# Retention and two feed-forward layers on one core: the order of the side work around the gated product's block products

## The chip, the cores and the metric

The kernel runs on one core of one Trainium2 chip. The metric is the device time of one execution in microseconds. Three runs of the kernel before took 1119.41 to 1124.32 us, with a median of 1120.45 us.

## The reference

A retention layer (linear attention whose state decays by a constant of each head) feeds two feed-forward layers, one with a leaky ReLU, one with a gate `h * sigmoid(1.702 h)`:

```python
for t in range(S):                       # S = 768, for 4 batches and 8 heads, head size 64
    state = gamma * state + einsum('bhd,bhe->bhde', k[:, :, t], v[:, :, t])
    y[:, :, t] = scale * einsum('bhd,bhde->bhe', q[:, :, t], state)
x = y.transpose(0, 2, 1, 3).reshape(3072, 512)
h = x @ moe_w_in;  x = maximum(0.01 * h, h) @ moe_w_out      # 512 -> 2048 -> 512
h = x @ moe2_w_in; x = (h * sigmoid(1.702 * h)) @ moe2_w_out
```

All is float32 in the result; the weights come in as float64 bit patterns and are made into float32 on the chip.

## The kernel before

Every value that TensorE multiplies stands as two parts, a rounded high part and a low part that is the rest, and each product is three matmuls (high by low, high by high, low by high). The order of the instructions on each engine is the order in which the program text issues them; no scheduler moves anything. Side work is put into a clock, `Later`: `at(ticks, step)` files a step, and each `tick()` at the end of a product runs the steps that are due.

The program has five stages, named here by the time at which the profiled execution is in them.

**Retention** (0 to 139 us) computes the first layer's input and the first of six token blocks of the first product.

**First product of the first layer** (139 to 356 us, `ffn_in`, L227): 5 blocks of 16 products, one tick each. Beside them 38 of 48 weight pieces are prepared. A `Prep` is one eighth-by-half of a weight matrix: it is loaded as 64-bit words; `words` makes float32 bits of them with two instructions on ScalarE (L167, L168) and four on VectorE (L169, L170, L172, L174); `sums` rounds (`round_up`, L178) and adds up three more block sums (L146); `store` writes seven blocks to DRAM. `Prep.start` files words, sums and store 3, 4 and 5 ticks behind the load. The raw words and the result take turns in three places.

**Second product of the first layer** (356 to 600 us, `Second`, L663): a Strassen-Winograd scheme with 7 block products instead of 8, in three token blocks of 56 items (7 products by 8 slices of the inner dimension). An item is 6 matmuls of 512 columns. Ahead of item n, `load` issues item n+13's data, `total` (L637) makes the operand sum of item n+5 on VectorE, `high` (L625, ScalarE) and `low` (L146, VectorE) split the operands of items n+4 and n+3. At the end of a product `evacuate` empties its PSUM banks: copies on ScalarE (L674, L684, L687, L704), sums on VectorE, and one sum on GpSimd (`other`, L671).

**Gated product, first of the second layer** (600 to 871 us, `First`, L497): the same scheme over 32 pairs (4 token blocks by 8 output slices); a pair is 7 block products of 6 matmuls with 384 columns, and a tick follows each product. For every pair ScalarE copies one accumulator to the other (L562), then a second one to SBUF (L568), and applies four sigmoids (L511); VectorE adds twice (L528) and multiplies four times (L515). The fourth product of a pair accumulates on the bank that L562 reads, and so waits for that copy. In the same stage stand `w_split` (L435, L146), which splits the weights of pairs 3 to 7, the remaining 10 `Prep`s (one at each even pair from 4 to 22), and for each new token block `early_sums` (L470, L471, on GpSimd) and seven `form`s (L483, L146).

**Second product of the second layer** (871 to 1121 us): `Second` again, with transposes of the results (L868).

What sets the order around the change is thus three tables: the ticks in `Prep.start`, the numbers in `LOADS, SUMS, HIGH, LOW`, and the pair and item numbers in `done1`, `step2`, `done2` and `done3`. The seven products of a pair that this document counts are those between two ticks of `First.run`.

## Time and profile before

| | |
|---|---|
| median of three runs | 1120.45 us |
| the profiled execution | 1122.98 us |
| its span, first to last instruction | 1121.3 us |
| mean granted TensorE clock | 0.987 |
| TensorE busy | 1070.3 us, 95% |
| VectorE busy | 835.0 us, 74% |
| ScalarE busy | 584.2 us, 52% |
| GpSimd busy | 74.3 us, 7% |

A row of the trace has the start of an instruction and its length in microseconds, its engine and line, and in square brackets the idle time of the engine before it and what ended that. In a table by stretches of time, the columns are the length of the stretch, the busy time of each engine with the count of its instructions, the granted TensorE clock as a share of full speed, the busy share of the DMA engines and what they moved. PEld is the load of weights into TensorE, which runs beside the matmuls.

### The profile page before, as it was taken

The numbers are of one execution on the slowest core, as the hardware profiler recorded it, in microseconds if no ns is written. First come the engines' busy times: TensorE is split into PE (matmuls) and PEld (weight loads), VectorE is DVE, ScalarE is ACT, GpSimd is POOL, SyncE is SP. The second block draws the span as 40 slices with busy tenths as digits, with TensorE's granted clock in tenths as the row PEclk, the third lists the DMA queues.
The fourth block names the chain that finished last, engine by engine and source line by source line (L and its number), as shares of the span: only waits on it lengthen the run. The fifth ranks groups of instructions, "written<-read, shape, count | busy, mean of one in ns | idle before, by whom it ended". The sixth has DMA issues, their size and how long they took to land.

```text
span 1121.3 us, 16864 instructions
## 1 busy us (share of the span) xinstructions
PE 1070.3 (95%) x6046; PEld 912.0 (81%) x6047; DVE 835.0 (74%) x1382; ACT 584.2 (52%) x1070; POOL 74.3 (7%) x45
## 2 busy tenths in 40 slices
PE   7999999999998999999988898988999999999997
PEld 5877788888887887878867897988899788888886
DVE  5988647977964887797887777585657897696784
ACT  5766444654556544545456553453556645545543
POOL 0211100000000000000023111011100000000000
PEclk9899999999999999999999999998999999999999
DMA  8899589998999328236255545454476725326322
GB/s 330 310 358 382 194 262 321 355 347 309 348 359 325 121 74 271 67 113 222 76 169 224 192 159 175 156 188 143 163 251 223 263 75 176 126 75 207 98 71 76
DMA packets 129636, 234.20 MB, mean 209 GB/s; under 512 B 11536, under 2 KB 69392, under 8 KB 126224
## 3 DMA queue, kind: packets, MB, share of 16 engines
q1 hardware_dynamic: 97152, 182.75, 48.3%
q10 hardware_dynamic: 32400, 50.38, 12.1%
q8 instruction: 47, 0.77, 0.3%
q14 instruction: 37, 0.30, 0.1%
HBM read 142.91 MB, written 90.18 MB: 208 GB/s over the span
## 4 chain that ended last, share of the span: by engine, by line
PE 74%; DVE 10%; DMA 7%; ACT 3%; issue 3%; POOL 1%; ACTq 1%; SPq 1%; DVEq 0%; POOLq 0%
PE psum L663 37%; PE psum L227 18%; PE psum L497 12%; PE psum L265 2%; DVE d L515 2%; DMA h<-qkv 2%; DMA h<-wd1o 2%; PE psum L295 1%; DMA h<-wd2o 1%; ACT h L435 1%; PE psum L868 1%; PE psum L288 1%; DVE c L146 1%; DVE e L146 1%; DMA gd<-d 1%
## 5 line engine op out<-in xcount | busy, mean ns | idle before, releaser
L663 PE MATMUL psum<-c,h 128*128 128x512 f32 x1008 | 232.5, 392 | 11.0 <-DVE c L146 11.0
L663 PEld LDWEIGHTS psum<-c,h 128*128 128x128 f32 x1008 | 189.7, 189 | 53.5 <-DVE c L146 14.2
L663 PE MATMUL psum<-e,h 128*128 128x512 f32 x810 | 192.5, 391 | 2.0 <-DVE e L146 2.0
L663 PEld LDWEIGHTS psum<-e,h 128*128 128x128 f32 x810 | 151.0, 188 | 34.7 <-DVE e L146 3.9
L497 PE MATMUL psum<-b,h 128*128 128x384 f32 x576 | 118.2, 351 | 19.0 <-ACT psum L562 18.6
L227 PE MATMUL psum<-d,h 128*128 128x512 f32 x576 | 135.9, 393 | 0.0
L227 PE MATMUL psum<-a,h 128*128 128x512 f32 x576 | 131.2, 389 | 0.0
L227 PEld LDWEIGHTS psum<-d,h 128*128 128x128 f32 x576 | 106.9, 188 | 24.8 <-issue 1.6
L227 PEld LDWEIGHTS psum<-a,h 128*128 128x128 f32 x576 | 108.0, 188 | 22.6 <-issue 0.2
L497 PEld LDWEIGHTS psum<-b,h 128*128 128x128 f32 x576 | 105.8, 198 | 23.5 <-ACT psum L562 23.5
L497 PE MATMUL psum<-c,h 128*128 128x384 f32 x576 | 112.1, 338 | 5.6 <-DVE psum L528 2.7
L497 PEld LDWEIGHTS psum<-c,h 128*128 128x128 f32 x576 | 102.0, 190 | 7.7 <-DVE psum L528 3.5
L511 ACT ACTIVATE d<-psum 128x384 f32<-128x384 f32 x96 | 47.2, 492 | 104.1 <-PE psum L497 58.2
L231 ACT ACTIVATE e<-psum 128x512 f32<-128x512 f32 x96 | 57.2, 595 | 80.3 <-PE psum L227 78.3
L625 ACT CAST c<-b 128x512 fp32r<-128x512 f32 x96 | 59.0, 622 | 67.7 <-DVE c L146 32.5
L146 DVE TENSOR_TENSOR h<-h 128x1024 fp32r<-128x1024 f32 (+3 forms) x51 | 52.5, 1037 | 48.5 <-ACT h L435 48.4
L146 DVE TENSOR_TENSOR c<-b,c 128x512 fp32r<-128x512 f32 x96 | 67.1, 702 | 14.8 <-ACT c L625 12.4
L625 ACT CAST e<-a 128x512 fp32r<-128x512 f32 x77 | 47.5, 622 | 51.5 <-DVE a L637 22.5
L146 DVE TENSOR_TENSOR e<-a,e 128x512 fp32r<-128x512 f32 x77 | 52.7, 688 | 14.5 <-ACT e L625 13.2
L435 ACT CAST h<-h 128x1024 fp32r<-128x1024 f32 (+3 forms) x51 | 45.2, 895 | 18.9 <-DMA h<-wd1o 4.2
L515 DVE TENSOR_TENSOR d<-psum,d 128x384 f32<-128x384 f32 x96 | 51.6, 551 | 4.5 <-ACT d L511 3.9
L663 PE MATMUL psum<-f,h 128*128 128x512 f32 x198 | 50.7, 391 | 0.0
(117 smaller groups left out, 1400.7 us busy)
## 6 DMA issues: line engine op xcount, KB each, us to landing
gd<-e ACTq DMA_DIRECT2D x96, 256.0 KB, 5.5
gd<-d ACTq DMA_DIRECT2D x128, 192.0 KB, 4.3
h<-qkv SPq DMA_DIRECT2D x21, 1024.0 KB, 7.6
b<-gd SPq DMA_DIRECT2D x72, 256.0 KB, 4.2
d<-gd SPq DMA_DIRECT2D x72, 256.0 KB, 4.5
a<-gd SPq DMA_DIRECT2D x48, 256.0 KB, 4.9
c<-w1i SPq DMA_DIRECT2D x16, 512.0 KB, 7.8
xd<-e SPq DMA_DIRECT2D x12, 512.0 KB, 3.1
```

The costliest lines, as they stand in the source:

```text
L146: e.tensor_tensor(out=o, in0=x, in1=y, op=ALU.subtract)
L227: nc.tensor.matmul(out=h, lhsT=w[:, a, k], rhs=xs[blk % 2][k][:, c], start=(i == 0), stop=(i == 3 * NP - 1), skip_group_check=True)
L231: nc.scalar.activation(out=t, in_=h, func=AF.Lrelu)
L265: nc.tensor.matmul(out=ps[:, e, n], lhsT=kT[r, n], rhs=qT[r, n], start=True, stop=True, skip_group_check=True)
L288: nc.tensor.matmul(out=kv[r, n], lhsT=ks[:, 2 * n + e], rhs=v[:, n, r], start=(c == 0 and n == 0), stop=True, skip_group_check=True)
L295: nc.tensor.matmul(out=out(n, e), lhsT=v[:, n, r], rhs=sm[:, e, n], start=(n < 2), stop=(c == 0), skip_group_check=True)
L435: nc.scalar.copy(out=hi.bitcast(F32R), in_=lo)
L497: nc.tensor.matmul(out=t, lhsT=w[:, k, a], rhs=x[:, b, k], start=(start and m == 0), stop=(m == 5), skip_group_check=True)
L511: nc.scalar.activation(out=s, in_=src, func=AF.Sigmoid, scale=1.702)
L515: nc.vector.tensor_tensor(out=dst, in0=src, in1=s, op=ALU.mult)
L625: nc.scalar.copy(out=t[:, 0], in_=self.block_of(*item))
L663: nc.tensor.matmul(out=t[:, j], lhsT=w[:, j, a], rhs=x[:, b], start=(new and q == 0 and m == 0), stop=(q == NQ - 1 and m == 2), skip_group ...
```

## The change

It touches five places.

1. In the gated product, weight splits and `Prep`s no longer run as whole steps of the clock. They are cut into pieces that stand in a queue, `behind`, and after each tick one piece is taken from it, except in a pair that forms operands of the next token block. A split is done by halves (`w_steps`), a `Prep` in six pieces (`steps`, `finish`), and its rounding and its three sums go from VectorE to GpSimd. Ten pairs are named for the ten `Prep`s.
2. In both second products the operand sums are issued from a table, `SUMS`, three in every four or five items, instead of eight in a row five items ahead. PSUM is emptied one to three items later than the end of its product, and the sum `other` moves from GpSimd to VectorE.
3. Six `Prep`s, those of the first three slices of the gated product's weights, are split when they are prepared, and both parts are stored (`wds`); their loads bring both parts, and they are not split again. All `Prep.start` ticks are one lower.
4. The operands of the gated product's first token block are formed a little earlier or later, with their sums on VectorE instead of GpSimd.
5. The last split of each second product stands at items 2 to 5 instead of 0 to 4, and by halves.

Where a `Prep` stands on VectorE in the gated product shows the first part. Here is VectorE before, from the `Prep` of pair 10 into pair 11 (pairs are counted from 0 to 31): L169 to L174 are `words`, L178 is `round_up`, the three L146 rows are the sums, and L528 and L515 are the pair's own adds and multiplies.

```order
L169 TENSOR_SCALAR e<-e 128x512
L170 TENSOR_SCALAR e<-e 128x512
L172 TENSOR_SCALAR e<-e 128x512
L174 SCALAR_TENSOR_TENSOR e<-e 128x512
L528 TENSOR_TENSOR psum<-psum,g 128x384
L178 ISA e<-e 128x1024
L146 TENSOR_TENSOR e<-e 128x256
L146 TENSOR_TENSOR e<-e 128x128 x2
L515 TENSOR_TENSOR d<-psum,d 128x384
L515 TENSOR_TENSOR d<-d 128x384
L515 TENSOR_TENSOR d<-psum,d 128x384 x2
```

And VectorE after, over pair 9, which has a `Prep` (L175 to L181 are the four `words`, L599 the adds, L586 the multiplies):

```order
L599 TENSOR_TENSOR d<-psum,g 128x384
L175 TENSOR_SCALAR e<-e 128x512
L177 TENSOR_SCALAR e<-e 128x512
L599 TENSOR_TENSOR psum<-psum,g 128x384
L586 TENSOR_TENSOR d<-psum,d 128x384
L586 TENSOR_TENSOR d<-d 128x384
L179 TENSOR_SCALAR e<-e 128x512
L181 SCALAR_TENSOR_TENSOR e<-e 128x512
L586 TENSOR_TENSOR d<-psum,d 128x384 x2
```

The pair's own instructions now stand between the words, one word to a tick, and the rounding and the sums are gone from VectorE.

They are on GpSimd, where before only the sums of the token blocks stood. GpSimd before, from the start of the gated product (L146 `form`'s sum, L470 and L471 `early_sums`):

```order
L146 TENSOR_TENSOR a<-a 128x768 x2
L470 TENSOR_TENSOR a<-a 128x768
L471 TENSOR_TENSOR a<-a 128x2x384
L146 TENSOR_TENSOR a<-a 128x768 x2
L470 TENSOR_TENSOR a<-a 128x768
L471 TENSOR_TENSOR a<-a 128x2x384
```

And after, from the third `Prep` before the second token block's sums (L190 is the rounding, L150 the sums of a `Prep` in tile e, L535 and L536 `early_sums`):

```order
L190 TENSOR_TENSOR e<-e 128x512
L150 TENSOR_TENSOR e<-e 128x256
L150 TENSOR_TENSOR e<-e 128x128 x2
L535 TENSOR_TENSOR a<-a 128x768
L536 TENSOR_TENSOR a<-a 128x2x384
L190 TENSOR_TENSOR e<-e 128x512
L150 TENSOR_TENSOR e<-e 128x256
L150 TENSOR_TENSOR e<-e 128x128 x2
L150 TENSOR_TENSOR a<-a 128x768 x2
```

A block's sums now queue behind the four GpSimd instructions of a `Prep` and before those of the next.

The third place is VectorE in the second product of the first layer, where the sixth product ends. Before (L637 an operand sum, L671 the emptying of PSUM, L146 `low`):

```order
L637 TENSOR_TENSOR b<-d,b 128x512
L671 TENSOR_TENSOR e<-psum,e 128x1024
L146 TENSOR_TENSOR c_3231<-b,c_3231 128x512
L637 TENSOR_TENSOR b<-d,b 128x512
L146 TENSOR_TENSOR c_3231<-b,c_3231 128x512
```

And after (L714 an operand sum, L748 the emptying, L150 `low`):

```order
L714 TENSOR_TENSOR b<-d,b 128x512
L748 TENSOR_TENSOR e<-psum,e 128x1024
L150 TENSOR_TENSOR c_3136<-b,c_3136 128x512
L748 TENSOR_TENSOR e<-e 128x1024
L150 TENSOR_TENSOR c_3136<-b,c_3136 128x512 x2
```

The operand sums are done before the emptying starts, and the sum that GpSimd made stands on VectorE one `low` later.

The diff, cut to its core:

```diff
...
+N_SPLIT = 3
...
@@ -410,30 +422,83 @@
             self.f, self.low = self.t[:, :4].rearrange("p b f -> p (b f)").bitcast(U32), raw[:, :, 0]
             words(self.f, self.low, raw[:, :, 1])
 
+        def total(self, e):
+            f = self.t
+            subtract(f[:, 4:6], f[:, :1].to_broadcast([P, 2, P]), f[:, 1:3], e)
+            t1, b22, b21 = (5, 1, 3) if self.kind == "2i" else (4, 2, 3)
+            subtract(f[:, 6], f[:, b22], f[:, t1], e)
+            subtract(f[:, 7], f[:, b21], f[:, 6], e)
+
         def sums(self):
             round_up(self.f, self.low)
-            f = self.t
-            subtract(f[:, 4:6], f[:, :1].to_broadcast([P, 2, P]), f[:, 1:3])
...
+            self.total(nc.vector)
...
+        def split(self):
+            self.hi = self.raw.bitcast(F32).rearrange("p b f t -> p (b f t)")[:, : 7 * P].rearrange("p (i f) -> p i f", i=7)
+            split(self.hi.bitcast(F32R), self.t[:, 1:].bitcast(F32R), self.t[:, 1:])
+
+        def store_split(self):
+            d = wds[:, self.q, self.hh]
+            nc.sync.dma_start(out=d[:, 0], in_=self.hi)
+            nc.sync.dma_start(out=d[:, 1], in_=self.t[:, 1:])
+
         def start(self, clock):
             self.load()
-            for ticks, step in ((3, self.words), (4, self.sums), (5, self.store)):
-                clock.at(ticks, step)
+            split = self.kind == "2i" and self.q < N_SPLIT
+            clock.at(2, self.words)
+            clock.at(3, self.sums)
+            if split:
+                clock.at(3, self.split)
+            clock.at(4, self.store_split if split else self.store)
+
+        def steps(self):
+
+            raw = self.raw.rearrange("p b f t -> p (b f) t")
+            self.t = next(self.rings[1])
+            self.f, self.low = self.t[:, :4].rearrange("p b f -> p (b f)").bitcast(U32), raw[:, :, 0]
+            out = [lambda: words_scalar(self.f, self.low, raw[:, :, 1])]
+            out += [lambda step=step: step(self.f, raw[:, :, 1]) for step in words_vector]
+            return out
...
+        def finish(self, clock, others):
+            round_up(self.f, self.low, nc.gpsimd)
+            self.total(nc.gpsimd)
+            clock.at(5, self.store)
+            if others:
+                others.pop(0).load()
...
-        nc.sync.dma_start(out=slot(q)[:, :, 1, a:b], in_=wd[kind][:, q, :, a:b])
+        if kind == "2i" and q < N_SPLIT:
+            nc.sync.dma_start(out=slot(q)[:, :, :, a:b], in_=wds[:, q, :, :, a:b])
+        else:
+            nc.sync.dma_start(out=slot(q)[:, :, 1, a:b], in_=wd[kind][:, q, :, a:b])
...
+    def w_parts(q, a, b, parts=None):
+
+        out = []
+        for hh in range(2):
+            t = slot(q)[:, hh].rearrange("p s i f -> p s (i f)")[:, :, a * P : b * P]
+            out.append((t[:, 0], t[:, 1]))
+        return out
 
     def w_split(q, a, b):
-        t = slot(q).rearrange("p h s i f -> p h s (i f)")[:, :, :, a * P : b * P]
-        hi, lo = t[:, :, 0], t[:, :, 1]
-        nc.scalar.copy(out=hi.bitcast(F32R), in_=lo)
-        subtract(lo.bitcast(F32R), lo, hi)
+        for hi, lo in w_parts(q, a, b):
+            split(hi.bitcast(F32R), lo.bitcast(F32R), lo)
+
+    def w_steps(q, a, b):
+        hi = lambda p: nc.scalar.copy(out=p[0].bitcast(F32R), in_=p[1])
+        lo = lambda p: subtract(p[1].bitcast(F32R), p[1], p[0])
+        u, v = w_parts(q, a, b)
+
+        def first():
+            hi(u)
+            hi(v)
+            lo(u)
+
+        return [first, lambda: lo(v)]
 
...
-        def run(self, done, step=lambda n: None):
+        def run(self, done, step, behind):
             later = self.clock
+
+            def tick():
+                later.tick()
+                if behind and self.free:
+                    behind.popleft()()
+
...
+                self.free = not (last or first_ or n == 0)
...
-                    later.tick()
+                    tick()
...
-    LOADS, SUMS, HIGH, LOW = 13, 5, 4, 3
+    LOADS, HIGH, LOW = 13, 4, 3
+    SUMS = {}
+    for blk in range(NB2):
+        for i, at in ((5, 0), (7, 11), (6, 22), (3, 31)):
+            for q in range(NQ):
+                SUMS.setdefault(7 * NQ * blk + at + 3 * q // 2, []).append((blk, i, q))
...
+                copy = lambda o, x: later.at(1, lambda: nc.scalar.copy(out=o, in_=x))
                 if i == 4:
                     kept[0] = new()
-                    nc.scalar.copy(out=kept[0], in_=bank["d"])
+                    copy(kept[0], bank["d"])
                 elif i == 5:
-                    put(kept[0], bank["e"], kept[0], ALU.subtract)
+                    later.at(2, lambda e=bank["e"], t=kept[0]: put(t, e, t, ALU.subtract))
...
-                    nc.scalar.copy(out=t, in_=bank["f"])
+                    copy(t, bank["f"])
                 elif i == 6:
-                    kept[1] = new()
-                    nc.scalar.copy(out=kept[1], in_=bank["f"])
-                    t = new()
-                    put(t, bank["d"], kept[1])
-                    result(blk, 1, 0, t, "d")
-                    k = kept.pop(0)
-
-                    def other():
-                        put(k, t, k, e=nc.gpsimd)
-                        result(blk, 1, 1, k, "d", 4)
-
-                    later.at(1, other)
+                    k, t = new(), new()
+                    kept[1] = k
+                    copy(k, bank["f"])
+                    later.at(2, lambda d=bank["d"]: put(t, d, k))
+                    result(blk, 1, 0, t, "d", 4)
+                    u = kept.pop(0)
+                    later.at(3, lambda: put(u, t, u))
+                    result(blk, 1, 1, u, "d", 6)
                 elif i == 3:
                     t = kept.pop(1)
-                    put(t, bank["e"], t)
-                    result(blk, 0, 1, t, "d")
+                    later.at(2, lambda e=bank["e"]: put(t, e, t))
...
-                for ahead, step in ((LOADS, self.load), (LOW, self.low), (SUMS, self.total), (HIGH, self.high)):
+                for ahead, step in ((LOADS, self.load), (HIGH, self.high), (LOW, self.low)):
...
+                for item in SUMS.get(n, ()):
+                    self.total(*item)
...
-        if n == 0:
-            w_split(7, 3, 7)
-        if n == 3:
-            w_split(7, 0, 3)
+        if n in (2, 3, 4, 5):
+            w_steps(7, *((3, 7) if n < 4 else (0, 3)))[n % 2]()
...
-        if m == 35:
+        if m == 33:
...
         if m == 40:
-            first2.early_sums()
-        if m in (42, 45, 47, 49):
-            first2.form(0, FORMS[{42: 0, 45: 1, 47: 2, 49: 3}[m]], (0, 2, 3) if m == 49 else (0, 1, 2), later)
+            first2.form(0, 1, (0, 0, 1), later)
+        if m == 43:
+            first2.early_sums(nc.vector)
+        if m in (45, 47, 49):
+            first2.form(0, {45: 5, 47: 2, 49: 6}[m], (0, 1, 2), later, nc.vector)
         if i == 6 and q == NQ - 1:
-            w_load("2i", 0, 3, 7)
-            later.at(5, lambda: w_split(0, 3, 7))
-        if i == 3 and q < 3:
-            if q:
-                w_load("2i", q, 3, 7)
-                later.at(5, lambda: w_split(q, 3, 7))
+            for u in range(3):
+                w_load("2i", u, 3, 7)
         if i == 3 and q == NQ - 1:
-            for u in range(2):
+            for u in range(3):
                 w_load("2i", u, 0, 2)
-                later.at(4, lambda u=u: w_split(u, 0, 2))
-        if i == 2 and q < 2:
+        if i == 2 and q < 3:
             w_load("2i", q, 2, 3)
-            later.at(4, lambda: w_split(q, 2, 3))
...
-    todo = names[N_IN1:]
+    todo = [Prep(*name, prep_rings2) for name in names[N_IN1:]]
+    behind, waiting = collections.deque(), []
...
-        if n == 0:
-            w_load("2i", 2, 0, 3)
-            later2.at(5, lambda: w_split(2, 0, 3))
         if n < 5:
             w_load("2i", n + 3, 0, 7)
         if 1 <= n <= 5:
-            w_split(n + 2, 3, 7)
-            later2.at(3, lambda: w_split(n + 2, 0, 3))
-        if 4 <= n < 24 and todo and n % 2 == 0:
-            Prep(*todo.pop(0), prep_rings2).start(later2)
+            behind.extend(w_steps(n + 2, 3, 7) + w_steps(n + 2, 0, 3))
+        if n in (4, 5):
+            todo[n - 4].load()
+        if n == 5:
+            waiting.extend(todo[2:])
+        if 6 <= n < 24 and n % NQ in (1, 2, 4, 5, 6) and todo:
+            p = todo.pop(0)
+            behind.extend([lambda: behind.extendleft(reversed(p.steps() + [lambda: p.finish(later2, waiting)]))])
...
-                later2.at(6, lambda: w_split(q, 3, 7))
-                later2.at(9, lambda: w_split(q, 0, 3))
+                later2.at(6, lambda: behind.extend(w_steps(q, 3, 7) + w_steps(q, 0, 3)))
...
-    first2.run(done2, step2)
+    first2.run(done2, step2, behind)
+    while behind:
+        behind.popleft()()
+    assert not todo
...
-        if n == 0:
-            w_split(7, 6, 7)
-        if n == 2:
-            w_split(7, 3, 6)
-        if n == 4:
-            w_split(7, 0, 3)
+        if n in (2, 4, 5):
+            w_split(7, *{2: (6, 7), 4: (3, 6), 5: (0, 3)}[n])
...
```

## Rows read from the trace of the kernel before

**Rows 1.** Table by stretches: the stages from 138.65 us on.

```profile
138.65:304.80 166.15, 166.15 (x733) 137.59 (x734) 126.93 (x283) 84.98 (x145) 0.00 (x0) 1.00 0.93 322
304.80:364.30 59.50, 55.76 (x247) 45.83 (x246) 35.19 (x59) 32.74 (x49) 0.00 (x0) 1.00 0.97 343
364.30:583.20 218.90, 215.03 (x936) 176.49 (x937) 179.54 (x262) 106.62 (x170) 12.03 (x5) 0.99 0.44 143
...
599.80:871.25 271.45, 246.87 (x1350) 240.24 (x1348) 186.57 (x322) 140.84 (x266) 25.23 (x15) 0.97 0.57 193
871.25:1116.00 244.75, 241.60 (x1107) 198.87 (x1106) 188.21 (x279) 124.66 (x194) 8.23 (x3) 1.00 0.40 129
```

**Rows 2.** TensorE's waits: line, what it waited for: us in total, times, longest.

```profile
PE psum L497 <- ACT psum L562: 18.6, 11, 3.5
```

**Rows 3.** Table by stretches: pairs 5, 13, 19, 23, 24 of the gated product.

```profile
637.49:650.21 12.72, 9.27 (x44) 8.79 (x43) 9.73 (x20) 5.07 (x10) 0.00 (x0) 0.87 0.44 139
...
712.18:720.98 8.80, 7.56 (x43) 7.24 (x43) 6.32 (x15) 2.75 (x6) 0.00 (x0) 1.00 0.59 190
761.15:775.70 14.55, 10.47 (x43) 9.83 (x43) 9.41 (x16) 2.75 (x6) 2.66 (x2) 0.77 0.38 123
799.06:808.02 8.96, 7.57 (x44) 7.25 (x44) 7.75 (x16) 4.84 (x9) 1.27 (x1) 1.00 0.38 140
808.02:815.30 7.28, 7.28 (x44) 7.28 (x44) 5.90 (x9) 4.32 (x8) 2.42 (x2) 1.00 0.30 109
```

**Rows 4.** Chain of work that ended last, in pair 13: start, us, what.

```profile
709.71 0.67 ACT e L167
...
711.66 0.69 DVE e L174
...
714.45 1.50 DVE d L515 x3
```

**Rows 5.** Instructions in order of time, from 762 us: start, us, engine, line.

```profile
762.00 1.89 POOL L471 TENSOR_TENSOR a<-a 128x768 f32<-128x768 f32 x1
...
762.24 2.20 DVE L174 SCALAR_TENSOR_TENSOR e<-e 128x512 uint32<-128x512 uint32 x1
```

**Rows 6.** GpSimd's groups: busy us, mean ns of one | idle before.

```profile
L146 POOL TENSOR_TENSOR h<-b,h 128x512 fp32r<-128x512 f32 x16 | 20.8, 1302 | 100.8 <-ACT h L149 100.8
...
L470 POOL TENSOR_TENSOR a<-a 128x768 f32<-128x768 f32 x4 | 7.4, 1851 | 123.1 <-DMA a<-xd 123.1
```

**Rows 7.** Instructions in order of time, from 587 us to 605 us.

```profile
587.01 4.37 PE L663 MATMUL psum<-c,h 128*128 128x512 f32 x18 [1.73 <-DVE c L146]
...
592.58 6.64 POOL L146 TENSOR_TENSOR a<-a 128x768 f32<-128x768 f32 x1 [14.25 <-DVE b L146]
...
605.02 2.37 PE L497 MATMUL psum<-b,h 128*128 128x384 f32 x12 [2.55 <-ACT psum L562]
```

**Rows 8.** Instructions in order of time, from 419 us to 424 us.

```profile
419.36 2.77 POOL L671 TENSOR_TENSOR e<-e 128x1024 f32<-128x1024 f32 x1 [291.62 <-DVE e L671]
...
419.80 2.88 DVE L637 TENSOR_TENSOR b<-d,b 128x512 f32<-128x512 f32 x1
...
423.34 3.02 PE L663 MATMUL psum<-c,h 128*128 128x512 f32 x12 [0.93 <-DVE c L146]
```

**Rows 9.** Chain of work that ended last, from 327 us to 350 us.

```profile
327.68 8.40 DMA wd2o<-b
...
343.37 7.08 DMA h<-wd1o
```

**Rows 10.** TensorE's next start, at 364 us.

```profile
364.29 15.96 PE L663 MATMUL psum<-c,h 128*128 128x512 f32 x62 [3.74 <-DVE c L146]
```

**Rows 11.** The DMA queue's own waits, 138 us to 356 us.

```profile
SPq L405 <- DVE b L178: 29.3, 12, 6.0
```

**Rows 12.** DMA issues, 600 us on: count, KB each, median us to landing.

```profile
h<-wd2i SPq DMA_DIRECT2D x5, 896.0 KB, 8.8
wd2o<-e SPq DMA_DIRECT2D x10, 448.0 KB, 2.9
```

More of the change, by code (lines that the diff above doesn't have):

```diff
@@ L1 @@
+import collections
 import itertools
@@ L465, in block, with early_sums, form @@
             return self.raw[:, 2 * c : 2 * c + 2, r * w : r * w + w]
-        def early_sums(self):
+        def early_sums(self, e=nc.gpsimd):
             a = self.block
-            nc.gpsimd.tensor_tensor(out=self.tmp, in0=a(1, 0), in1=a(1, 1), op=ALU.add)
-            nc.gpsimd.tensor_tensor(out=a(1, 0), in0=a(1, 0), in1=a(0, 0), op=ALU.subtract)
-        def form(self, blk, i, at=(0, 2, 3), clock=None):
+            e.tensor_tensor(out=self.tmp, in0=a(1, 0), in1=a(1, 1), op=ALU.add)
+            e.tensor_tensor(out=a(1, 0), in0=a(1, 0), in1=a(0, 0), op=ALU.subtract)
+        def form(self, blk, i, at=(0, 2, 3), clock=None, e=nc.gpsimd):
             clock = clock or self.clock
@@ L569, in run @@
                     form(5)
-                    later.tick()
+                    tick()
                 if old:
@@ L574, in run @@
                     form(7)
-                    later.tick()
+                    tick()
                 if now:
@@ L579, in run @@
                     form(2)
-                    later.tick()
+                    tick()
                     product(cur["b"], n, 6, False)
@@ L583, in run @@
                     form(6)
-                    later.tick()
+                    tick()
                 if old:
@@ L588, in run @@
                     form(3)
-                    later.tick()
+                    tick()
                     product(old["b"], n - 1, 4, False)
@@ L593, in run @@
                     done(*pairs[n - 1])
-                    later.tick()
+                    tick()
             later.drain()
-    LOADS, SUMS, HIGH, LOW = 13, 5, 4, 3
+    LOADS, HIGH, LOW = 13, 4, 3
[4 more added lines that the diff above has]
+                SUMS.setdefault(7 * NQ * blk + at + 3 * q // 2, []).append((blk, i, q))
     ITEMS = [(blk, i, q) for blk in range(NB2) for i in ORDER2 for q in range(NQ)]
```

33 lines of the change are left out of this document (19 added, 14 removed).

## The prediction

> **What bounds the kernel now.** I read the table by stretches first. TensorE is busy in 95% of the span, and in the first product it does not pause at all: 166.15 of 166.15 us, while the DMA engines are busy for 0.93 of the time. In the gated product it is busy in 246.87 of 271.45 us at a mean granted clock of 0.97, and the weight loads (PEld, 240.24) fill what is left [rows 1]. That stage can be measured without any busy time: pair 24, in which nothing is late, takes 7.28 us at full clock [rows 3], so a product takes 1.04 us, and the stage's 224 products 233.0 us. The stage is 38.5 us longer than that.
>
> Next come TensorE's waits: in this stage nearly all, 18.6 us in 11 waits, are for ScalarE's copy L562 [rows 2]. Pair by pair, the lateness has one owner. The ten odd pairs from 5 to 23, each behind a pair that starts a `Prep`, take from 8.80 to 14.55 us; four of them, the first, the last and the extremes, and the clean pair are shown [rows 3]. Over 7.28 us they are late by 5.4, 1.5, 3.8, 5.7, 1.5, 1.6, 2.2, 7.3, 1.5 and 1.7 us, 32.2 in sum. Of the other pairs, the first is about 2.9 late (a wait of 2.55 is in it, [rows 7]) and the rest about 3.4 together.
>
> The chain of waits in pair 13 shows how: a `Prep`'s words start at 709.71, VectorE works through words, rounding and sums, and comes to the multiplies of the pair only at 714.45 [rows 4]. ScalarE's sigmoids wait for these multiplies to free their tiles, and L562 stands behind the sigmoids. So 4.74 us of VectorE without a gap cost the pair 1.5 us; it bears about 3.2. In pair 19 GpSimd's sums fell into the words as well: beside a GpSimd instruction of 1.89 us L174 took 2.20 [rows 5] instead of 0.69 [rows 4]. With some 3.1 us more of this the pair lost 7.3 instead of 1.5, since TensorE's granted clock in it was 0.77, against 1.00 in pair 13 [rows 3]: behind a pause of several us it came back at the lower of its two levels, 1.2 GHz, for part of the time. A us beyond the 4.74 thus cost about 1.85 us.
>
> **The change, part by part**, against the profiled execution's 1122.98 us, 1.7 of which lie around the span.
>
> *`Prep`s in pieces.* The four words stand in four ticks, each of 0.42 to 0.69 us beside 0.46 to 1.1 us of the pair's own work in a tick of 1.04. VectorE's longest stretch without a gap drops from 4.74 to about 2 us, below the 3.2 that a pair bears. The rounding and the sums go to GpSimd, which is idle here but for the token blocks' sums. The trace has no integer add on GpSimd. The nearest row is a float sum of the same 512 elements, 1.30 us, and 768 elements take 1.85 [rows 6]; so the three sums, with 512 elements in all, are about 1.7 more, and a `Prep` about 3.0 us. From below the bound is VectorE's own instruction, 0.7; from above GpSimd's longest, 6.64 us for 768 elements [rows 7]. I take 1.30, the row of the same size. The store comes 5 ticks, 5.2 us, behind it: nothing waits for it but the `Prep` after the next, and 448 KB land in 2.9 us [rows 12]. If VectorE had to wait out all 3.0, that alone would still be under 3.2.
>
> One pair stays exposed: in pair 14 a token block's two sums (1.85 and 1.89) come on GpSimd right behind the `Prep` of pair 13, while pair 14's own words run. As in pair 19 two words would wait some 1.6 us each; with 2 us of words that makes about 5 us, and by the slope above 2 us of loss. I leave 3.0 of the 32.2 for this pair and small things: **29.2 gained**.
>
> The row says that VectorE waits for a GpSimd instruction that reads SBUF. The Trainium skill (SBUF — State Buffer, section "Who interferes with whom") has this as a lock: a VectorE instruction with two SBUF inputs, or in a two-port mode, and a GpSimd instruction take the shared ports in turn, and the second waits for the whole of the first. Rows 5 agree: 2.20 is close to 1.89 plus what was left of L174. By the lock no single VectorE instruction waits longer than one GpSimd instruction, 1.30 here, and the ten pairs would leave less than 3.0; counted as 3.0 us in a row for every `Prep` they would still be within 3.2, and the sum changes by under 3 us either way.
>
> *Splits in pieces, and the start of the gated product.* The splits of pairs 3 to 7 become two instructions each per engine. The waits in pairs 1 to 4 are about 1.1 us. But pair 1 now uses the first of these weights sooner: its load of 896 KB needs 8.8 us [rows 12], and ScalarE asks for it some 5.4 us into the stage, where in the trace the late start gave it time. I put 1.5 us there in place of 1.1. The wait of 2.55 for L562 in pair 0 comes from the chain of operand forms behind GpSimd's sum of 6.64 us [rows 7], which goes to VectorE at about 1 us. Of 2.9 I leave 0.5. Together with pair 29: **2.0 gained**.
>
> *End of the first second product.* Three waits of 1.7 us (one of them in rows 7) and a small one, 5.2 us, fall where splits, forms and `low`s crowd on VectorE. The splits of three slices vanish there (both parts come by DMA), and the added sums on VectorE are four of about 1 us. I leave 0.7: **4.5 gained**.
>
> *Sums spread, `other` on VectorE.* At the end of the sixth product GpSimd's 2.77 us held three operand sums up to 2.88 us, and TensorE waited 0.93 [rows 8]; the same a block later, 1.0. After, the instruction costs VectorE about 1.3 us where no operand sum is left. A `low` is 3 items ahead, 4 us, which hides it. In the last stage TensorE is busy for 241.60 of 244.75 us [rows 1], so there the move has nothing to gain. **1.9 gained**. The later emptying delays no bank: each is written again 7 items later or more.
>
> *Start of the first second product.* TensorE waits 3.74 us at its fourth item [rows 10], and the chain behind it is DMA: the last `Prep`'s store (8.40), then loads, then the weights that ScalarE splits (7.08) [rows 9]. Now the ticks are one lower, 2.7 us (61 products in 166.15 us, [rows 1]). Against it six `Prep`s store 448 KB more each, 2.7 MB, 8.3 us at 322 GB/s, in a stage whose DMA engines have 7%, 11.6 us, to spare [rows 1]; and the next load into a place must wait until that store has landed, on a queue that already waits for places, 29.3 us in all [rows 11]. Two rounds of three such `Prep`s may put the queue some 10 us back, with 16 more `Prep`s to catch up. From 2.7 gained to 8 lost; I take **0**. TensorE itself has six banks of slack there, about 14 us.
>
> *Start of the last stage*: splits a little later, **0.5 gained**.
>
> Sum: 29.2 + 2.0 + 4.5 + 1.9 + 0 + 0.5 = 38.1, so 1122.98 - 38.1 = 1084.9 for an execution like the profiled one. That one was 2.5 us over the median of the runs; I say **1084 us**.
>
> **The rivals.**
>
> *Everything clears.* Pair 14, pair 1 and the 3.74 go too: some 10 us better, 1074. For it speaks that a clean pair sits next to every late one; against it the two collisions above.
>
> *The split stores set the queue back.* The loads of 139 to 340 us end later, and the fourth item waits 8 to 10 us more: 1093. For it, 0.93 and 29.3 us; against it, that the last loads have 16 `Prep`s' time to recover.
>
> *GpSimd's rounding takes twice the float sum or more.* With 3.0 us instead of 1.30, a `Prep` holds GpSimd 4.7 us; if VectorE waits it out, each of the ten pairs again loses 1.5: 1100.
>
> *The slower case* is the same mechanism further on: an integer add far slower than a float one. The gain of 38.1 is gone when each pair loses 3.8, which by the slope is 6.0 us of hold, a rounding of 4.3 us. At 5 us each pair loses 5.1, and the time is 1136. Against it: no GpSimd sum in the trace is this slow except when another instruction held it [rows 7].
>
> *It does not do what it says*: another side instruction, ScalarE's words (1.3 us in one piece), takes the place of the burst. L562 comes five ticks later, so I see no way to more than 1105.
>
> **How the numbers follow.** Forecast 0.58, with 1078 to 1090 of its own; everything clears 0.13; split stores 0.12; twice the rounding 0.08; words on ScalarE 0.04; slower 0.05. The range runs from the best case's lower side to beyond the split stores' 1093 and to the 1100 of the fourth: 1071 to 1103. What a measurement tells from no change is about 0.5%, 5.6 us: faster needs less than 1114.8. The first five cases are all below that, but some of the last ones' spread is not: faster 0.90, same 0.05, slower 0.05.
>
> **What would show it.** In the profile after, pairs of the gated product take 7.3 us throughout, pair 14 perhaps 9, the stage about 239 us instead of 271, the granted clock there 1.00; waits for L562 are under 4 us; GpSimd's rounding is near 1.3 us. The waits at the ends of the sixth product are gone. The wait at the fourth item of the first second product is the term that I trust least. I am wrong if `Prep` pairs still take over 8.5 us, or if the first product (166 us without a pause) shows pauses.

## The result and the profile after

The changed kernel takes 1093.96 us (median of four runs, 1091.57 to 1096.75) against 1120.3 us before (also four runs): a ratio of 0.976, 95% interval 0.972 to 0.980. It is 2.4% faster, and 10 us above the forecast of 1084. The profiled execution took 1092.11 us, its span 1090.4.

The stretches are those of [rows 1]. The second starts at the same time as there, 304.80 us, in the fourth of the first product's five blocks; the others are cut at the same events: the start of the first product's five blocks, the restart of the second product at its fourth item, the gated product and the last stage. Columns: length, busy time of PE, PEld, DVE, ACT and POOL, granted clock, DMA share, GB/s.

```profile
138.59:304.80 166.21, 159.57 (x695) 129.73 (x696) 119.02 (x257) 78.00 (x133) 0.00 (x0) 1.00 0.89 306
304.80:377.09 72.29, 64.78 (x285) 52.98 (x283) 50.27 (x105) 43.21 (x81) 0.00 (x0) 0.97 1.00 353
377.09:603.40 226.31, 226.31 (x992) 187.28 (x993) 188.11 (x283) 114.40 (x181) 2.18 (x1) 0.99 0.47 156
603.40:838.43 235.03, 234.08 (x1348) 233.44 (x1347) 168.14 (x300) 142.17 (x284) 54.39 (x54) 1.00 0.63 221
838.43:1085.40 246.97, 241.01 (x1107) 199.04 (x1106) 185.99 (x287) 125.58 (x199) 0.00 (x0) 1.00 0.39 128
```

Read the ends of the stretches against those of before. The restart moves from 364.29 to 377.09, 12.8 us later. From there to the gated product it takes 226.3 us instead of 235.5, 9.2 less. The gated product falls from 271.45 [rows 1] to 235.03, 36.4 less. The last stage, to the end of the span, goes from 250.05 to 251.97, 1.9 more. The four differences add up to -30.9, the difference of the two spans.

TensorE's waits after, over the whole run (total, times, longest):

```profile
PE psum L740 <- DVE c L150: 7.5, 2, 7.3
PE psum L239 <- ACT e L243: 5.1, 5, 1.8
PE psum L740 <- DVE f L150: 3.0, 1, 3.0
PE psum L239 <- DVE d L150: 2.1, 2, 1.4
PE psum L740 <- DVE e L150: 1.9, 1, 1.9
PE psum L568 <- ACT psum L634: 0.7, 1, 0.7
PE psum L568 <- DVE d L599: 0.3, 1, 0.3
```

The 18.6 us for the accumulator's copy in the gated product [rows 2] have become 0.7 (L634 is that copy now). But the first product, L239, whose last five blocks ran without a pause before, waits 7.2 us, 6.6 of them in these five blocks, and the wait at the fourth item [rows 10] has grown from 3.74 to 7.3. TensorE comes to the second product at 365.03 us; before, the row was

```profile
356.31 4.24 PE L663 MATMUL psum<-c,h 128*128 128x512 f32 x18
```

So 8.7 of the 12.8 us arise in the first product, and nearly all the rest in that wait. TensorE's rows around the restart, and at the start of the last stage:

```profile
365.03 2.88 PE L740 MATMUL psum<-c,h 128*128 128x512 f32 x12
368.11 1.67 PE L740 MATMUL psum<-c,h 128*128 128x512 f32 x6 [0.20 <-DVE c L150]
377.09 23.15 PE L740 MATMUL psum<-c,h 128*128 128x512 f32 x95 [7.31 <-DVE c L150]
...
844.61 1.65 PE L740 MATMUL psum<-e,h 128*128 128x512 f32 x6 [1.89 <-DVE e L150]
849.22 1.66 PE L740 MATMUL psum<-f,h 128*128 128x512 f32 x6 [2.96 <-DVE f L150]
```

**Where the 12.8 us come from.** The six split `Prep`s store at 235.36 to 266.99 us, 6.3 us apart. Two of them on ScalarE (L153 is the split's copy, L171 the next `Prep`'s words, L243 a leaky ReLU of the first product):

```profile
247.08 0.94 ACT L153 CAST b<-b 128x896 fp32r<-128x896 f32 x1 [2.90 <-DVE b L150]
...
248.98 0.66 ACT L171 ACTIVATE b<-b 128x512 f32<-128x512 f32 x1 [0.46 <-ACT e L243]
...
253.60 0.94 ACT L153 CAST b<-b 128x896 fp32r<-128x896 f32 x1 [2.90 <-DVE b L150]
254.45 0.66 ACT L171 ACTIVATE c<-c 128x512 f32<-128x512 f32 x1
...
255.58 0.57 ACT L243 ACTIVATE e<-psum 128x512 f32<-128x512 f32 x1
```

and on VectorE (L190 the rounding, L150 first the sums and then the split's subtract, L175 the next words):

```profile
251.76 0.69 DVE L190 CUSTOM_DVE_ANT_0 b<-b 128x1024 uint16<-128x1024 uint16 x1
252.49 1.08 DVE L150 TENSOR_TENSOR b<-b 128x256 f32<-128x256 f32 x3
254.57 1.09 DVE L150 TENSOR_TENSOR b<-b 128x896 fp32r<-128x896 f32 x1 [1.01 <-ACT b L153]
255.58 0.42 DVE L175 TENSOR_SCALAR c<-c 128x512 uint32<-128x512 uint32 x1
```

Sums, copy and subtract stand in one tick. ScalarE comes to the copy early and stands there 2.90 us until VectorE has the sums; the next `Prep`'s words and the leaky ReLUs of the first product are queued behind it. VectorE then stands 1.01 us for the copy, and the next words reach it only when ScalarE is through. The two engines wait for each other in turn, six times. But waits are only a part of it: the subtract is 1.09 us of new work on VectorE for each such `Prep`, in whatever order it stands. The Trainium skill (PSUM — Partial Sum Buffer, section "Engine vs sequencer instructions") says that the queues of ScalarE and VectorE are strictly first in, first out; these rows agree. The words at 254.45 read place c, whose loads were issued by 245.0; the loads of this stretch landed at most 5.6 us after their issue, so by 250.7 they could have run, and they stand behind the copy until 254.45.

### The profile page after: what moved, and what is told of

It is laid out like the page before. It is cut to its first block, busy times and chain, and to the rows that moved or that the text cites. A ratio compares the mean times of both kernels' runs of the same rounds, so it can differ in the third digit from the quotient of the medians.

```text
span 1090.4 us, 16958 instructions
## 1 busy us (share of the span) xinstructions
PE 1056.0 (97%) x6047; PEld 903.7 (83%) x6047; DVE 815.5 (75%) x1392; ACT 588.3 (54%) x1111; POOL 78.7 (7%) x76
## 3 DMA queue, kind: packets, MB, share of 16 engines
q10 hardware_dynamic: 32400, 50.38, 12.5%
## 4 chain that ended last, share of the span: by engine, by line
PE 78%; DMA 10%; DVE 5%; ACT 4%; issue 2%; SPq 1%; ACTq 0%; DVEq 0%
PE psum L740 41%; PE psum L568 21%; PE psum L239 10%; DMA h<-wd1o 2%; PE psum L277 1%; DMA b<-w1o 1%; PE psum L307 1%; DMA h<-qkv 1%; DMA b<-gd 1%; DMA c<-w1o 1%; DMA b<-w2i 1%; PE psum L942 1%; ACT e L243 1%; PE psum L300 1%; DMA c<-w1i 1%
## 5 line engine op out<-in xcount | busy, mean ns | idle before, releaser
L239 PE MATMUL psum<-d,h 128*128 128x512 f32 x576 | 137.0, 394 | 3.8 <-DVE d L150 2.1
L239 PE MATMUL psum<-a,h 128*128 128x512 f32 x576 | 132.2, 390 | 3.5 <-ACT e L243 3.5
L239 PEld LDWEIGHTS psum<-d,h 128*128 128x128 f32 x576 | 106.4, 188 | 30.1 <-DVE d L150 3.0
L239 PEld LDWEIGHTS psum<-a,h 128*128 128x128 f32 x576 | 107.8, 188 | 27.3 <-ACT e L243 4.7
L568 PE MATMUL psum<-b,h 128*128 128x384 f32 x576 | 110.3, 334 | 0.7 <-ACT psum L634 0.7
L568 PEld LDWEIGHTS psum<-b,h 128*128 128x128 f32 x576 | 100.7, 188 | 1.0 <-ACT psum L634 1.0
L243 ACT ACTIVATE e<-psum 128x512 f32<-128x512 f32 x96 | 56.8, 592 | 47.6 <-PE psum L239 41.4
L150 DVE TENSOR_TENSOR c<-b,c 128x512 fp32r<-128x512 f32 x96 | 65.5, 689 | 18.2 <-ACT c L702 16.0
L150 DVE TENSOR_TENSOR h<-h 128x384 fp32r<-128x384 f32 (+2 forms) x86 | 51.0, 628 | 29.2 <-ACT h L153 19.0
L150 DVE TENSOR_TENSOR e<-a,e 128x512 fp32r<-128x512 f32 x77 | 52.3, 688 | 18.5 <-ACT e L702 17.1
L586 DVE TENSOR_TENSOR d<-psum,d 128x384 f32<-128x384 f32 x96 | 51.4, 548 | 3.6 <-ACT d L582 3.0
L150 POOL TENSOR_TENSOR a<-a 128x768 f32<-128x768 f32 x7 | 13.2, 1888 | 487.1 <-DMA h<-wds 471.9
```

What stands on the lines that cost most here:

```text
L150: e.tensor_tensor(out=o, in0=x, in1=y, op=ALU.subtract)
L239: nc.tensor.matmul(out=h, lhsT=w[:, a, k], rhs=xs[blk % 2][k][:, c], start=(i == 0), stop=(i == 3 * NP - 1), skip_group_check=True)
L243: nc.scalar.activation(out=t, in_=h, func=AF.Lrelu)
L568: nc.tensor.matmul(out=t, lhsT=w[:, k, a], rhs=x[:, b, k], start=(start and m == 0), stop=(m == 5), skip_group_check=True)
L586: nc.vector.tensor_tensor(out=dst, in0=src, in1=s, op=ALU.mult)
```

## The experiments

Twelve kernels, three timed rounds each beside the kernel before; times are medians of four runs. Beside these kernels the kernel before took 1122.2 to 1123.6 us, against 1120.3 beside the changed kernel, so a difference of some 3 us from the changed kernel says nothing. "Restart" is the fourth item of the first second product in the profiled execution (before 364.3, after 377.1).

**1. Without the six split `Prep`s** (no_split_store).

```diff
-            split = self.kind == "2i" and self.q < N_SPLIT
+            split = False
...
                 w_load("2i", u, 3, 7)
+                later.at(5 + 2 * u, lambda u=u: w_split(u, 3, 7))
```

> The changed kernel without the six split Preps: all 2i Preps store one word per number, and the three slots are split by ScalarE and VectorE at the end of the first second product. Theory (the six split Preps set the queue back, so that the first second product restarts at its fourth item at 377.1 us instead of 364.3): the first product runs its 166 us without the five waits for ScalarE, the restart lies at 364 to 367 us, the program takes 1082 to 1086 us. Rival, ticks (the steps of every Prep are due one tick earlier, words before their load has landed): the pauses and the restart stay within 2 us of the changed kernel, 1091 to 1095. Third, the twelve splits that come back at the end of the second product cost what they save: restart early, but waits of 5 us or more at 580 to 600, 1088 or more.

1082.61 us (1080.63 to 1084.32), 11 us below the changed kernel. No pause in the first product, and:

```profile
362.44 29.34 PE L740 MATMUL psum<-c,h 128*128 128x512 f32 x126 [0.52 <-DVE c L150]
...
586.17 3.01 PE L740 MATMUL psum<-c,h 128*128 128x512 f32 x12 [1.81 <-DVE c L150]
```

The restart is 14.7 us earlier, and earlier even than before; the splits that come back at the end cost the wait of 1.81 us. The split `Prep`s are the cause of the later restart. Here the same six `Prep`s store 3.80 us apart (234.15 to 253.16), VectorE going from one to the next without a gap: that pace is its own work. The changed kernel's 6.33 is 2.53 more, 12.6 us over the five steps, most of the 14.7. By its rows VectorE has 1.09 us of the 2.53 for the subtract, stands 1.01 for the copy and some 0.4 for ScalarE's words. So under half is the split's own work on VectorE, and the rest is waiting.

**2. The same with the old ticks** (no_split_old_ticks): words, sums and store at 3, 4, 5.

```diff
-            clock.at(2, self.words)
-            clock.at(3, self.sums)
+            clock.at(3, self.words)
+            clock.at(4, self.sums)
```

> The same without split Preps, and words, sums and store due at 3, 4 and 5 ticks again instead of 2, 3 and 4. Theory (split Preps alone): within 2 us of the run without split Preps, since loads have landed by either tick; the restart at 364 to 367 us. Rival (ticks): 4 us or more faster than that run, which itself stays near 1093. A small gain of the earlier tick, which the prediction put at 2.7 us at most, would show as 1 to 3 us slower than the run without split Preps.

1083.17 us (1081.11 to 1087.74), restart 364.4. In the two profiled executions the restart differs by 1.9 us; the time differs by nothing that can be measured.

**3. The split's copy on VectorE** (hi_on_vector).

```diff
-            split(self.hi.bitcast(F32R), self.t[:, 1:].bitcast(F32R), self.t[:, 1:])
+            nc.vector.tensor_copy(out=self.hi.bitcast(F32R), in_=self.t[:, 1:])
+            subtract(self.t[:, 1:].bitcast(F32R), self.t[:, 1:], self.hi)
```

> The changed kernel with the six split copies on VectorE, right behind its own sums, instead of on ScalarE; stores, bytes and places as in the changed kernel. Theory A1 (ScalarE stands in its order behind VectorE's sums, and the activations of the first product and the words of the next Prep behind it): the waits of TensorE for ScalarE in the first product (5.1 us) vanish, Preps follow at about 4.5 us, the restart lies near 368 us, 1084 to 1088 us. Rival A2 (the two stores of 0.9 MB together hold the place of the next load): pauses and restart within 3 us of the changed kernel's, 1091 to 1095.

1089.80 us (1088.70 to 1095.27). Neither theory fits the whole: the median is 4.2 us lower, with ranges that overlap, but in the profiled execution, the longest of the four, the restart lies at 377.7 and the first product still waits 4.6 us. ScalarE no longer waits for the sums, but VectorE has 5.6 us of work for each such `Prep` (their stores come 5.90 us apart), and SyncE's loads now wait for the split's stores:

```profile
SPq L414 <- DMA wds<-b: 12.9, 4, 4.1
SPq L414 <- DMA wds<-c: 6.4, 2, 3.7
```

In the changed kernel these waits are 4.8 and 2.6 us. One wait has taken the other's place, so this run does not tell what the order alone costs.

**4 and 5. The bytes without the split.** Six extra stores of 0.45 MB, from the `Prep`s' own results (extra_bytes_only) or from a tile that nothing waits for (extra_bytes_free_place).

```diff
-            nc.sync.dma_start(out=d[:, 0], in_=self.hi)
-            nc.sync.dma_start(out=d[:, 1], in_=self.t[:, 1:])
+            self.store()
+            nc.sync.dma_start(out=d[:, 1], in_=self.t[:, 1:])
```

and in the second kernel, for the last line,

```diff
+            nc.sync.dma_start(out=d[:, 1], in_=home["h1"].view(60, 7, P).bitcast(F32))
```

> The run without split Preps, but the six Preps still issue two stores from the same places (the second copy is never read), so that the bytes written in the first product are those of the changed kernel, without the split's work on ScalarE and VectorE. Rival A2 (bytes and held places): restart at 373 to 377 us, 1090 to 1094 us. Theory A1 (ScalarE's order): restart at 364 to 368 us, 1082 to 1087 us, like the run without split Preps.

> The run without split Preps, with the same six extra stores (0.45 MB each, never read) as the run with extra bytes, but taken from a finished tile of weights that nothing waits for, so that the bytes are moved and no place of the Preps is held longer. In the run with extra bytes from the Preps' own places the restart of the second product lay at 373.25 us against 362.44 without them. Theory (the place that each split Prep holds while two stores land makes the next load late): restart at 362 to 366 us, 1082 to 1085 us. Rival (the bytes themselves, since DMA is 0.90 to 0.95 busy there): restart at 370 us or later, 1087 to 1092 us.

1087.62 us (1085.86 to 1094.48) and 1087.21 us (1085.95 to 1090.31). The first one's profile is of its 1094.48 run, so its restart of 373.3 stands for that run only; the second's profiled run is near its median:

```profile
367.79 31.38 PE L738 MATMUL psum<-c,h 128*128 128x512 f32 x126 [5.59 <-DVE c L150]
```

By the medians the bytes cost about 4.8 us over experiment 1, wherever they are taken from. The theory that the result's place is held is not borne out, though the restart of 367.79 lies between the two forecasts; and the first product waits 0.6 us at most: bytes alone don't make the pauses. Neither kernel holds the place of the raw words, in which the changed kernel's high parts lie until they are stored; the next experiment has no such store either, and answers that.

**6. The split's work without its bytes** (split_work_one_store); the stored words are the low parts alone.

```diff
-            clock.at(4, self.store_split if split else self.store)
+            clock.at(4, self.store)
```

> The changed kernel with the six split copies and subtracts of the Preps still done on ScalarE and VectorE, but with the single store of every other Prep, and the three slots split again at the end of the first second product; the stored words of the six Preps are the low parts alone, so the work has the right amount and the numbers do not. Runs so far: 1082.6 without split Preps, 1087 with their extra bytes alone, 1094 with both. Theory (bytes and split work each cost about half, the work because ScalarE stands in its order behind VectorE's sums): TensorE waits 3 to 5 us for ScalarE in the first product, restart at 366 to 371 us, 1086 to 1090 us. Rival (the work costs only where the bytes have already made the queue late): no pauses, restart at 362 to 365 us, 1082 to 1084 us.

1097.07 us (1095.90 to 1100.40), later than either theory said: the work alone, with one store and no place held longer, makes the whole shift. PE's and ScalarE's waits (ScalarE's from 232 to 300 us), and the restart:

```profile
PE psum L239 <- ACT e L243: 3.0, 4, 1.3
PE psum L239 <- DVE d L150: 2.1, 2, 1.3
```

```profile
ACT b L153 <- DVE b L150: 11.6, 4, 2.9
ACT c L153 <- DVE c L150: 6.7, 2, 3.3
```

```profile
376.18 24.21 PE L740 MATMUL psum<-c,h 128*128 128x512 f32 x94 [7.33 <-DVE c L150]
```

ScalarE's 18.3 us in six waits are those of the changed kernel, to the tenth. Bytes (4.8) and work (14.5 over experiment 1) don't add up to the changed kernel's 11.4. The changed kernel saves the splits at the end, 2.3 us; beyond that, why the two do not add is not shown.

**7. The gated part alone, on the kernel before** (gated_alone): `behind`, `w_steps`, `steps` and `finish`, nothing else.

> The kernel before with the gated product's part of the change alone: side work one piece per block product, rounding and sums of the last ten Preps on GpSimd. Theory (the parts are separate in time): all 28 even and odd pairs at 7.3 us, the gated stage 235 us for 271, the other stages as before, 1083 to 1088 us in all. Rival (the clean gated product needs the earlier parts' changes): pairs 1 to 4 or the last stage lose 5 us or more, 1090 or above.

1091.55 us (1087.84 to 1095.24), above the theory, in the rival's range but not for its reason. The profiled execution's gated product:

```profile
602.20:841.02 238.82, 235.86 (x1348) 235.01 (x1347) 172.20 (x307) 144.05 (x291) 56.82 (x55) 0.99 0.63 220
```

32.6 us less than before. The 3.8 that are missing against the changed kernel come from pair 0: TensorE still waits 2.67 us there for the copy, as in [rows 7], and its matmuls then take 1.8 us more at a granted clock of 0.99 over the stage. The last stage takes 2.4 us more than before. So this part alone gives as much as the whole change, whose other gains are eaten by its split `Prep`s and its last stage.

**8 and 9. Engine or pieces.** Ten bursts, rounding and sums on GpSimd (burst_on_gpsimd); single pieces, all on VectorE (pieces_on_vector).

```diff
-            behind.extend([lambda: behind.extendleft(reversed(p.steps() + [lambda: p.finish(later2, waiting)]))])
+            def burst():
+                for piece in p.steps():
+                    piece()
+                p.finish(later2, waiting)
+
+            behind.append(burst)
```

```diff
-            round_up(self.f, self.low, nc.gpsimd)
-            self.total(nc.gpsimd)
...
+            return [lambda: round_up(self.f, self.low),
+                    lambda: subtract(f[:, 4:6], f[:, :1].to_broadcast([P, 2, P]), f[:, 1:3]), last]
```

> The changed kernel with each of the ten late Preps handled as one burst: both ScalarE words and all four VectorE words behind one block product, then GpSimd's rounding and sums; engines as in the changed kernel, only the single pieces are undone. Theory (most of the 3.2 us per odd pair was VectorE's nine instructions in a row, and the move of five of them to GpSimd takes half of it away, the pieces the other half): the ten pairs take 8.0 to 9.5 us, the gated stage 242 to 255 us, 1101 to 1114 us in all. Rival (the move to GpSimd alone does it): pairs at 7.3 to 7.6 us, time within 3 us of the changed kernel's 1094. Second rival (pieces alone): pairs at 10 us or more, 1120.

> The changed kernel with the rounding and the sums of the ten late Preps back on VectorE, still one piece per block product (eight pieces for a Prep where GpSimd's five instructions were one). Theory (a single VectorE instruction of 0.7 us per block product fits into what VectorE has free there, so that pieces alone clear the pairs): gated stage 235 to 237 us, time within 2 us of the changed kernel's 1094. Rival (GpSimd's relief is needed): pairs at 7.6 to 8.5 us, stage 240 to 250 us, 1099 to 1109. With bursts on GpSimd the stage took 244.2 us.

1106.14 us (1102.25 to 1111.15) and 1095.87 us (1095.73 to 1100.44). The gated product of each:

```profile
604.20:848.40 244.20, 236.07 (x1349) 233.18 (x1348) 168.06 (x300) 140.84 (x284) 57.40 (x54) 1.00 0.61 213
```

```profile
606.50:841.60 235.10, 234.15 (x1348) 233.49 (x1347) 179.39 (x340) 141.53 (x284) 23.85 (x14) 1.00 0.64 221
```

In pieces the stage is clear on either engine; bursts with GpSimd's relief leave 9 us, as the theory of experiment 8 said. Bursts with all of the work on VectorE were not run in this kernel. A burst of half the length still hurts, and the longest of ten such waits on VectorE shows why:

```profile
671.86 0.43 DVE L175 TENSOR_SCALAR e<-e 128x512 uint32<-128x512 uint32 x1 [2.15 <-ACT e L171]
```

VectorE stands 2.15 us for ScalarE's words of the same tick, and the pair's own work behind it: two engines in one tick, as in experiment 6. The ten waits are 12.5 us; in pieces, where ScalarE's words are one product ahead, experiment 9 has a single one of 0.5 us.

**10. PSUM emptied at once, the other sum on GpSimd** (emptied_at_once), on the kernel of experiment 1: `evacuate` as before.

```diff
-                copy = lambda o, x: later.at(1, lambda: nc.scalar.copy(out=o, in_=x))
-                    copy(kept[0], bank["d"])
+                    nc.scalar.copy(out=kept[0], in_=bank["d"])
```

> The run without split Preps (1082.6 us; the first second product takes 228.6 us from its fourth item to its end, 235.5 in the kernel before), with PSUM emptied at once at the end of each product, as in the kernel before, and the other sum on GpSimd again. Theory (most of the 6.9 us comes from spreading the operands' sums, the later emptying gives about 2): 229 to 232 us for that stretch, 1083 to 1088 us. Rival (the later emptying gives most): 233 us or more, and waits of 1 us or more again at the product ends, 1088 to 1093.

1087.34 us (1086.45 to 1087.54). From the restart to the gated product 233.68 us instead of 228.58: later emptying, together with `other` on VectorE, gives 5.1 us there, most of what that stretch gained. The rival holds for that stretch, while the time lies in the theory's range; the waits are many and small (nine with that at the restart, 5.6 us, 1.0 the longest).

**11. Operand sums eight in a row again** (sums_in_a_row), on the same kernel.

```diff
+    for k, item in enumerate(ITEMS):
+        SUMS.setdefault(max(k - 5, 0), []).append(item)
```

> The run without split Preps with every operand's sum five items ahead again, so eight in a row for each product that has one, and emptying still late. Theory (the sums in a row were what made VectorE late at the product ends): 232 to 236 us from the fourth item of the first second product to its end, waits for VectorE's subtract at the ends of products 4 to 6, 1087 to 1094 us over both second products, less 2 us where the last stage starts, since no sum then stands at its first item. Rival (the late emptying had made room enough): 228 to 230 us, 1080 to 1084 us.

1078.90 us (1078.49 to 1080.83), lower than experiment 1 by 3.7, so the theory falls. Restart to gated product takes 228.72 us: the spread gave 0.1. The spread costs at the start of the last stage, where the waits, 2.6 and 2.7 us in experiment 1, are now 2.6 and 0.2:

```profile
833.89 1.66 PE L738 MATMUL psum<-e,h 128*128 128x512 f32 x6 [2.63 <-DVE e L150]
...
842.58 1.66 PE L738 MATMUL psum<-f,h 128*128 128x512 f32 x6 [0.23 <-DVE f L150]
```

**12. Put together** (best): experiment 1, the first block's sums of product 5 at items 3 to 10, and the third slot's splits in the gated product's first pair.

```diff
+                n = at + 3 * q // 2 if i != 5 or blk else q + 3
...
+            later2.at(4, lambda: w_split(2, 0, 3))
```

> The changed kernel without split Preps (1082.6 us when run), with two more edits: the third slot's weights are split in the first pair of the gated product instead of at the crowded end of the second product, and the first block's sums of product 5 in both second products stand at items 3 to 10 instead of 0 to 10. Theory (in the last stage VectorE's first sum waits 3.1 us for its load, and the third item's subtract stands behind it): the two waits of TensorE at the start of the last stage fall from 5.4 to 2.7 us, the wait of 1.8 us at the end of the first second product goes, 1077 to 1080 us. Rival (the weights' splits set that start, not the sum): both waits stay, 1081 to 1083 us.

1080.52 us (1077.92 to 1081.14), ratio to before 0.961 (0.958 to 0.964): better than both kernels, 0.5 us above the theory's range. The two waits at the last stage's start fall to 2.1 and 0.5 us, as expected; the 1.8 us at the end of the second product stay, which was a miss. Experiment 11 stands at 0.961 (0.960 to 0.963): no difference between the two. Sums in a row together with the third slot's move was not run. Nor was a split one tick behind the sums with its store a tick later: its high parts lie in the place that the next load takes at that tick.

## Why the prediction was right or wrong

**Gated product (29.2 and most of 2.0): right in place, too small.** 36.4 us came where some 31 were forecast. From pair 2 on every pair but the last takes 7.28 us, and the stage's granted clock is 1.00. Pair 14's collision happened: VectorE's words beside the token block's sum on GpSimd,

```profile
707.93 2.06 DVE L177 TENSOR_SCALAR e<-e 128x512 f32<-128x512 f32 x1
```

```profile
707.68 2.02 POOL L535 TENSOR_TENSOR a<-a 128x768 f32<-128x768 f32 x1
```

2.06 us for an instruction of 0.42, but in single pieces the pair bore it. The Trainium skill (SBUF — State Buffer, section "Who interferes with whom") names `tensor_scalar` among the operations that can enter a two-port mode and so take the shared ports. Whether this one did, the row doesn't show, but it agrees: it ends at 709.99 us, 0.29 after GpSimd's 709.70. It moved no time. GpSimd's rounding took what the sum assumed:

```profile
L190 POOL TENSOR_TENSOR e<-e 128x512 int32<-128x512 int32 x10 | 13.1, 1306 | 89.5 <-ACT d L582 74.3 <-DVE e L181 11.8 <-DMA e<-w2o 3.4
```

1.306 us beside the float sum's 1.302 [rows 6]; both rivals on a slow rounding are out. But the reason was only half right: I gave GpSimd a share in it, and experiment 9 shows that it is not needed once the work stands in pieces. I also read 4.74 us of VectorE without a gap in [rows 4]. The first 0.69 of them are ScalarE's words, and VectorE stood still:

```profile
710.40 0.43 DVE L169 TENSOR_SCALAR e<-e 128x512 uint32<-128x512 uint32 x1 [1.62 <-ACT e L167]
```

VectorE's own stretch was 4.05 us, and before it stood the wait between two engines that experiment 8 shows again.

**End of the first second product and sums (4.5 and 1.9): 9.2 came for 6.4, partly for another reason.** Of it 2.3 us are the splits that are gone (226.3 against 228.6 in experiment 1), 5.1 the later emptying together with `other` on VectorE, 0.1 the spread of the sums; no run tells where the other 1.7 come from. What of the 5.1 belongs to `other`, the row behind the term of 1.9, is not separated; for the spread the term was wrong.

**Start of the first second product (0): the step that failed.** It measured +12.8, beyond its own bound of 8. The bound counted DMA time and held places, [rows 9, 11], and experiments 4 and 5 give the bytes only some 5 us. It put the split's work at nothing, and experiment 6 shows the whole shift with that work alone: for each `Prep` 1.09 us of subtract on VectorE, and waits of two engines on each other, since in one tick the split's copy waits for the sums, and the subtract and the next words for the copy. How much another order would give back is not shown. I also wrote that six banks of slack cover TensorE; the first product paused 6.6 us. The prediction named that as a sign of being wrong, and the wait at the fourth item as its least trusted term.

**Start of the last stage (0.5 gained): wrong in sign, 1.9 lost.** The table puts the first sums at item 0, before their data has landed, and `low` stands behind:

```profile
847.87 0.69 DVE L714 TENSOR_TENSOR a<-b,a 128x512 f32<-128x512 f32 x1 [3.32 <-DMA b<-gd]
```

Experiments 11 and 12, which ask for that sum later, take 2.5 to 2.8 us off.

**The rivals.** "Everything clears" happened in the gated product and "the split stores set the queue back" at the restart, both at once, which no rival was. That rival's 1093 is the measured time, but by the split's work more than by its stores.

**The sum.** Part of its nearness is luck: the terms that came too small, by some 8 us in all, hide half of the 15 us by which the other two were missed. And 38.1 off the profiled 1122.98, less the 2.5 by which that execution lay over the median, is 1082.4, not the 1084 that I said.

## What to carry to other kernels

Be wary of putting an instruction and the one on another engine that it needs into the same place of the order: here the engine that came early stood there, 2.90 us on ScalarE and 2.15 on VectorE, with all that was queued behind it. Price a moved step by its own time on the engine that sets the pace and by the chain across the engines, not by its bytes alone. And cutting a burst into single pieces can be worth more than moving it to an idle engine.

## What was not expected of the hardware

The spread of four runs differs much from kernel to kernel: 8.6 us in experiment 4 (1085.86 to 1094.48), 8.9 in experiment 8, 7.4 in experiment 7, but 1.1 in experiment 10. What sets it is not shown: extra bytes do not explain it, since experiment 5 has as many as experiment 4 and spreads 4.4 us, and experiment 7 has none.
